# Gated recurrence, then a mixture of experts on one core: experts taken in order with fixed addresses, a branch for the fourth tile, and a new order in the recurrence

## The chip, the cores and the metric

One core of a Trainium2 chip. The metric is the time of one execution on the device in microseconds (us), the median of several runs. Engines are named as in the profile: PE (TensorE matmul), PEld (its weight loads), DVE (VectorE), ACT (ScalarE), POOL (GpSimd), SP (SyncE, which here only issues DMAs). A name with q (SPq, PEldq) is the engine's instruction queue.

## What is computed

Two blocks, one behind the other; everything is 32-bit float.

```python
# recurrence: B=4, H=8, S=768, D=48
f = sigmoid(f_logit)
state = f[t, :, None] * state + outer(k[t], v[t])     # per batch and head
y[t]  = q[t] @ state
# x = y as (B*S, H*D) = (3072, 384)
logits = x @ w_gate                                   # 8 experts
e      = argmax(logits);  gate = softmax(logits)[e]
out    = gate * (relu(x @ w1[e]) @ w2[e])             # F = 1024
```

The inputs come from a fixed seed. Routing them by the reference gives 406, 413, 352, 385, 335, 443, 396 and 342 tokens for experts 0 to 7. In tiles of 128 tokens that is 4, 4, 3, 4, 3, 4, 4 and 3: 29 tiles, five of them fourth ones.

## The kernel before, in words

**Recurrence.** Twelve units (`NU`), each 128 time steps of two batches with all heads, two chains of six. The order on every engine is written out by hand (`manual_schedule`). In iteration `n` of the loop (L434) unit `n` is scored (`score`: PE matmuls, then DVE copies under the causal mask, L298), its keys are transposed (`keys`), the state's increment is made (`added`, PE) and taken up (`update`, DVE and POOL). Unit `n-1` gets its outputs (`within` for the unit's own steps, `before` for the old state, both PE). Unit `n-2` is carried out (`settle`: ACT copies from PSUM; `rows`: PE transposes it and multiplies by the gate's weights, ACT and DVE copy the results). Ahead of that run the gates: `growth(n+2)` (ACT exponent, POOL add), `product(n+2)` (a DVE scan, L258), `by_r(n+1)` (POOL multiplies the keys, L269), `log_r` and `decay` (ACT, with a table load each), `by_decay(n+1)` (DVE, L283). SP loads f, k, q and v of unit `n+3` into one of three buffers each (`ld`, `bufs=3`). The PSUM pool `pst` has two slots, which `xp`, `kp`, `rp` and `dp` take in turn.

**Routing.** Every second iteration, for four chunks of 128 tokens (for two chunks at the end), `Route` chooses the expert (`choose`, DVE), counts by matmul (`count`, PE), computes each token's row in its expert's region (`place`, DVE) and sends four blocks of rows by indirect DMA from POOL to the DRAM array `xs` (`send`, L149).

**Between.** L499 and L500 read a flag on all five engines and branch over a slow fallback that does not run with these inputs. Then SP writes a block of padding rows behind the last token of each expert (L575, L576), while DVE works out a plan of 31 tiles (`NT`, L586 to L615): for each tile its expert and its first row. Tiles that are not needed read a dummy block.

**Experts.** 31 tiles: SP reads expert and row from the plan (L624, L625), loads the rows (`xrow`, L627) and the expert's whole `w1` (`w1t`, 1.5 MB, L629; every tile anew). PE transposes the rows (L633), does 24 matmuls with `w1` (L644; the trace shows 48, two for each in 32-bit float), ACT and DVE each do the relu of one half (L652, L654), PE does 8 matmuls with `w2` (L658; 16 in the trace), reading its expert from a register that L655 loads. DVE scales by the gate (L662) and POOL scatters the rows to the output (L149). All eight `w2` lie in SBUF, loaded during the recurrence. Here the order on the engines is the scheduler's.

Of the kernel before, what the change touches and what calls it, by code (L numbers as in the profile page):

```python
# [19 lines left out]
C = 128  # L20
# [16 lines left out]
DUMMY = E * REGION  # L37
ROWS = DUMMY + C

# [6 lines left out]
NT = N // C + E - 1  # L46
# [5 lines left out]
def _consts():  # L52
# [3 lines left out]
    def row(v):  # L56
# [8 lines left out]
        "eidx": row(e),  # L65
        "tiles": row(np.arange(N // C) * C),
        "i": row(np.arange(NT)),
        "irow": row(np.arange(NT) * C - DUMMY),
# [8 lines left out]
    f["rows"] = sel.reshape(128, HP * XW)  # L77
    m = {"causal": np.triu(np.ones((128, 128)))}
# [17 lines left out]
def kernel(  # L96
# [34 lines left out]
    w2r = cpool.tile([128, E, NF, DM], F32, name="w2r")  # L131
    base = cpool.tile([128, B * NC + 1, E], F32, name="base")
# [12 lines left out]
    nc.scalar.dma_start(xs[DUMMY : DUMMY + C], pad)  # L145
    nc.vector.tensor_copy(base[:, 0], const("first"))
# [14 lines left out]
    class Route:  # L161


        def __init__(self, pool, lg, bases, xr, toks, group):
            self.pool, self.lg, self.bases = pool, lg, bases
            self.xr, self.toks, self.group = xr, toks, group
            self.n = lg.shape[1]
# [22 lines left out]
        def place(self):  # L190
            n, bases, rp = self.n, self.bases, self.rp
            at = self.t("place", E)
            nc.vector.tensor_copy(at[:, 0], bases[0])
# [4 lines left out]
            nc.vector.tensor_tensor(at, rp[:, 0], at, op=OP.add)  # L198
            nc.vector.tensor_tensor(at, at, self.oh, op=OP.mult)
            pos = self.t("pos")  # L200
            nc.vector.reduce_sum(pos, at, axis=AX_X)
            self.posi = self.pool.tile([128, n], I32, name="posi")
            nc.vector.tensor_copy(self.posi, pos)
# [4 lines left out]
        def send(self):  # L208
# [4 lines left out]
            nc.gpsimd.tensor_copy(self.xr[:, :, TOK], self.toks)  # L213
            for c in range(self.n):
                scatter(xs, self.posi[:, c : c + 1], self.xr[:, c, :], ROWS - 1, self.group)


    ordered = {getattr(mybir.EngineType, n) for n in ENGINES}
    with ExitStack() as st:
        ld = st.enter_context(tc.tile_pool(name="ld", bufs=3))  # L220
# [8 lines left out]
        nc.vector.memset(cap[:, :, 0:1], 1.0)  # L229

        scores = [wk.tile([128, 2, 2, HP, C], F32, name=f"at{i}", bufs=1) for i in range(2)]
        for t in scores:
            nc.vector.memset(t, 0.0)
# [4 lines left out]
        def load(u, *names):  # L238
            x = units[u]
            for n in names:  # L240
# [5 lines left out]
                nc.sync.dma_start(x[n], src[u])  # L246

        def growth(u):

            f = units[u]["f"]  # L250
# [3 lines left out]
        def product(u):  # L254

            x = units[u]
            x["r"] = wk.tile([128, SEG, CR], F32, name="r", bufs=1)
            nc.vector.tensor_tensor_scan(  # L258
                x["r"].rearrange("p s c -> p (s c)"),
                x["f"].rearrange("p s c -> p (s c)"),  # L260
                cap.rearrange("p s c -> p (s c)"),
# [5 lines left out]
        def by_r(u):  # L267
            x = units[u]
            nc.gpsimd.tensor_tensor(x["k"], x["k"], x["r"][:, :, 1:CR], op=OP.mult)  # L269
            nc.gpsimd.tensor_copy(rend[:, u], x["r"][:, :, C])  # L270

        def log_r(u):
            x = units[u]
            nc.scalar.activation(x["f"][:, :, 1:CR], x["r"][:, :, 1:CR], AF.Ln)

        def decay(u):
            x = units[u]
            x["dec"] = x["f"][:, :, 1:CR]
            nc.scalar.activation(x["dec"], x["dec"], AF.Exp, scale=-1.0)  # L279

        def by_decay(u):
            x = units[u]
            nc.vector.tensor_tensor(x["q"], x["q"], x["dec"], op=OP.mult)  # L283
# [80 lines left out]
        def update(u):  # L364
# [3 lines left out]
            last = x["dec"][:, :, C - 1 : C].to_broadcast([128, SEG, D])  # L368
# [15 lines left out]
        def rows(u):  # L384
# [3 lines left out]
            if u == g[0]:  # L388
                n = 2 * len(g)
                group["xr"] = wk.tile([128, n, ROW], F32, tag="xr", name="xr")  # L390
                group["lg"] = wk.tile([128, n, E], F32, tag="lg", name="lg")
                nc.gpsimd.memset(group["xr"][:, :, USED:ROW], 0.0)
# [16 lines left out]
            if u != g[-1]:  # L409
                return None  # L410
            n = 2 * len(g)
            b0 = 2 * (g[0] % 2)
            toks = const("tok").rearrange("p (b c) -> p b c", c=NC)[:, b0 : b0 + n, g[0] // 2]
            return Route(
                wk,
                group["lg"],
                [base[:, 2 * g[0] + j] for j in range(n + 1)],
                group["xr"],
                toks,
                "xs",  # L420
            )

        st.enter_context(tc.manual_schedule(engines=ordered))
        for u in range(3):
            load(u, *"fkqv")
        growth(0)
        product(0)
        by_r(0)
        log_r(0)
        decay(0)  # L430
        by_decay(0)
        growth(1)
        product(1)
        for n in range(NU + 2):  # L434
# [7 lines left out]
            if n + 1 < NU:  # L442
                by_r(n + 1)
                log_r(n + 1)
            if 0 <= last:
# [23 lines left out]
            if here < NU and here // 2 < NC - 1:  # L469
                update(here)  # L470
            if rt:
                rt.send()
            if n + 2 < NU:
                product(n + 2)
            if 0 <= back < NU:
                before(back)
            if n + 3 < NU:
                load(n + 3, *"fkqv")
            if 1 <= n <= E:
                e = n - 1  # L480
                nc.sync.dma_start(w2r[:, e], moe_w2[e].rearrange("(f p) d -> p f d", p=128))
# [14 lines left out]
        nc.vector.tensor_copy(end, base[:, B * NC])  # L496
# [3 lines left out]
    with tc.If(flag > 0):  # L500
        with ExitStack() as st:
            gp = st.enter_context(tc.tile_pool(name="gp", bufs=1))
            gps = st.enter_context(tc.tile_pool(name="gps", bufs=1, space=PSUM))
            nc.vector.tensor_copy(end, const("first"))
            wg3 = gp.tile([128, KD, E], F32, name="wg3")
# [42 lines left out]
            with tc.For_i(0, B) as b:  # L548
                with tc.For_i(0, S, C) as c:
# [13 lines left out]
                    rt = Route(gp, lg, [end, end], xr, toks, None)  # L563
                    rt.choose()
                    rt.count(gps.tile([128, 2, 1, E], F32, name="grp"))
                    rt.place()
                    rt.weigh()
                    rt.send()
# [5 lines left out]
    for e in range(E):  # L574
        row = nc.sync.value_load(endi[:, e : e + 1], min_val=e * REGION, max_val=e * REGION + N)  # L575
        ins = nc.sync.dma_start(xs[ds(row, C)], pad).ins  # L576
        tc.declare_no_dep(ins, group="xs", reason="no row is written twice")
        tc.add_to_no_dep_group("xs", ins)


    def p_tile(name, *shape):
        return cpool.tile([1, *shape], F32, name=name)

    one = slice(0, 1)
    cnt = p_tile("cnt", E)
    nc.vector.tensor_tensor(cnt, end[one], const("first")[one], op=OP.subtract)  # L586
    more = p_tile("more", E, N // C)
    nc.vector.tensor_tensor(  # L588
# [131 lines left out]
```

## Time and profile before

| what | us |
| --- | --- |
| median of three runs | 593.29 |
| lowest, highest | 588.04, 596.0 |
| the profiled execution | 593.54 |
| its span in the profile | 591.8 |

The span runs from the first to the last instruction in the trace; the profiled execution's own time is 1.74 us longer. Mean granted TensorE clock over the span: 0.932 of full speed.

### The profile page before, as it was taken

The page shows a single profiled execution, that of the slowest core. Times are in us where ns is not written, and L with a number is a line of the kernel's source. Part 1 is how long each engine was busy: PE and PEld are TensorE (multiplying, and loading weights), DVE is VectorE, ACT ScalarE, POOL GpSimd, SP SyncE. Part 2 cuts the span into 40 slices and gives each one's busy share as a digit, 9 for nine tenths or more (in the row PEclk, how much of TensorE's full clock was granted, in tenths as well). Part 3 has the DMA queues.
Part 4 walks back from the last instruction along what each step waited for, and adds up shares of the span by engine and source line. Part 5 has one row for each costly group of instructions (what it writes and reads, how often), then busy time and mean ns, then how long its engine had stood idle before and what let it go on. Part 6 is the DMA issues. An engine that isn't in the chain of part 4 may idle for free.

```text
span 591.8 us, 9687 instructions
## 1 busy us (share of the span) xinstructions
PE 485.2 (82%) x3803; PEld 396.2 (67%) x3803; DVE 177.0 (30%) x373; ACT 126.0 (21%) x172; POOL 115.2 (19%) x121
## 2 busy tenths in 40 slices
PE   0777957879684049999999999999999999999995
PEld 0767857868574047667867877778667767786683
DVE  5756646667544201112011111110211111202110
ACT  5577546665531001000000000000000000000000
POOL 3333625472723000001000100010001000100010
PEclk9888969979898559999999999999999999999998
DMA  8555686887602483434553555345434544554300
GB/s 336 199 191 215 211 343 208 330 309 251 247 34 77 147 331 115 154 135 138 195 191 126 155 201 177 135 163 191 168 129 157 195 177 135 157 205 162 135 10 0
DMA packets 37665, 105.57 MB, mean 178 GB/s; under 512 B 3806, under 2 KB 17153, under 8 KB 37616
## 3 DMA queue, kind: packets, MB, share of 16 engines
q1 hardware_dynamic: 33248, 94.55, 45.6%
q0 software_dynamic: 3520, 9.64, 4.2%
q10 hardware_dynamic: 848, 0.71, 0.4%
q8 instruction: 32, 0.52, 0.4%
q14 instruction: 17, 0.14, 0.1%
HBM read 93.41 MB, written 12.85 MB: 180 GB/s over the span
## 4 chain that ended last, share of the span: by engine, by line
issue 56%; POOL 5%; PE 2%; SPq 2%; DMA 1%; POOLq 0%; DVE 0%
POOL out_dram L149 5%; PE hps L644 1%; DMA xrow<-xs 1%; PE yps L658 1%; SPq L575 1%; SPq L576 1%; SPq L625 0%; POOLq L149 0%; SPq L624 0%; POOLq L715 0%; SPq L627 0%; SPq L629 0%; DVE ysb L662 0%; DVE more L588 0%; DVE nt L592 0%
## 5 line engine op out<-in xcount | busy, mean ns | idle before, releaser
L644 PEld LDWEIGHTS hps<-xT,w1t 128*128 128x128 f32 x1488 | 172.3, 194 | 21.4 <-DVE xT L635 11.3
L644 PE MATMUL hps<-xT,w1t 128*128 128x128 f32 x1488 | 175.3, 278 | 13.5 <-DVE xT L635 7.8
L658 PE MATMUL yps<-w2r,hT 128*128 x496 | 170.0, 490 | 12.7 <-DVE hT L654 12.5
L658 PEld LDWEIGHTS yps<-w2r,hT 128*128 128x128 f32 x496 | 90.3, 190 | 76.7 <-DVE hT L654 24.4
L149 POOL DMA_INDIRECT out_dram<-ysb,dst x31 | 30.3, 978 | 364.7 <-DVE ysb L662 324.9
L652 ACT ACTIVATE hT<-hps 128x512 f32<-128x512 f32 x31 | 18.5, 597 | 335.5 <-PE hps L644 335.5
L637 DVE CAST dst<-xrow 128x1 int32<-128x1 f32 x31 | 4.8, 154 | 209.3 <-DMA out_dram<-ysb,dst 193.7
L662 DVE TENSOR_SCALAR ysb<-yps,xrow 128x384 f32<-128x384 f32 x31 | 19.1, 617 | 99.2 <-PE yps L658 99.2
L295 PE MATMUL s<-q,k 64*128 64x128 f32 x384 | 28.1, 303 | 19.6 <-DVE q L283 19.6
L295 PEld LDWEIGHTS s<-q,k 64*128 64x128 f32 x384 | 25.8, 211 | 21.3 <-issue 20.6
L258 DVE TENSOR_TENSOR_SCAN r<-f,cap 128x1032 f32<-128x1032 f32 x12 | 32.4, 2703 | 10.1 <-POOL f L252 10.1
L310 PE MATMUL kp<-fpack,k 128*128 128x128 f32 x96 | 18.4, 351 | 20.8 <-DVE lg L404 20.8
L319 PE MATMUL yt<-at,v 128*64 128x128 f32 x384 | 32.0, 328 | 0.0
L397 PE MATMUL xp<-fpack,ys 128*128 128x104 f32 x192 | 26.1, 292 | 7.2 <-ACT ys L380 7.2
L149 POOL DMA_INDIRECT xs<-xr,posi x24 | 26.2, 1094 | 26.1 <-DVE xr L212 13.7
L298 DVE COPY_PREDICATED at<-mpack,s 128x1024 f32<-128x1024 uint8 x24 | 29.6, 1287 | 1.6 <-PE s L295 1.6
L397 PEld LDWEIGHTS xp<-fpack,ys 128*128 128x128 f32 x192 | 24.0, 203 | 9.0 <-ACT ys L380 8.1
L269 POOL TENSOR_TENSOR k<-k,r 128x1024 f32<-128x1024 f32 x12 | 26.2, 2187 | 18.6 <-DVE r L258 14.0
L310 PEld LDWEIGHTS kp<-fpack,k 128*128 128x128 f32 x96 | 14.4, 180 | 23.2 <-DVE lg L404 22.6
L633 PE MATMUL etp<-fpack,xrow 128*128 128x128 f32 x93 | 13.2, 278 | 20.4 <-issue 20.4
L319 PEld LDWEIGHTS yt<-at,v 128*64 128x64 f32 x384 | 27.1, 169 | 3.0 <-issue 2.7
L283 DVE TENSOR_TENSOR q<-q,f 128x1024 f32<-128x1024 f32 x12 | 15.0, 1247 | 44.7 <-ACT f L279 44.7
(81 smaller groups left out, 314.5 us busy)
## 6 DMA issues: line engine op xcount, KB each, us to landing
w1t<-in_moe_w_dram SPq DMA_DIRECT2D x31, 1536.0 KB, 8.1
w2r<-in_moe_w_dram SPq DMA_DIRECT2D x8, 1536.0 KB, 10.0
xrow<-xs SPq DMA_DIRECT2D x31, 200.0 KB, 2.4
f<-in_fu_dram SPq DMA_DIRECT2D x12, 516.0 KB, 7.3
k<-in_ku_dram SPq DMA_DIRECT2D x12, 512.0 KB, 7.9
q<-in_qu_dram SPq DMA_DIRECT2D x12, 512.0 KB, 5.6
v<-in_vu_dram SPq DMA_DIRECT2D x12, 512.0 KB, 5.7
xs<-pad SPq DMA_DIRECT2D x8, 200.0 KB, 1.9
```

What stands on the lines that cost most here:

```text
L149: ins = nc.gpsimd.indirect_dma_start(out=dst, out_offset=bass.IndirectOffsetOnAxis(ap=idx, axis=0), in_=src, in_offset=None, bounds_check= ...
L258: nc.vector.tensor_tensor_scan(x["r"].rearrange("p s c -> p (s c)"), x["f"].rearrange("p s c -> p (s c)"), cap.rearrange("p s c -> p (s c) ...
L269: nc.gpsimd.tensor_tensor(x["k"], x["k"], x["r"][:, :, 1:CR], op=OP.mult)
L295: nc.tensor.matmul(ps[:, h, p], lhsT=x["k"][r, s], rhs=x["q"][r, s], start=True, stop=True)
L298: nc.vector.copy_predicated(x["at"][:, a].rearrange("p h s c -> p (h s) c"), _bc(causal, 1, SEG), ps.rearrange("p h s c -> p (h s) c"),)
L310: nc.tensor.transpose(kp[:, p], x["k"][:, HP * a + p], ident)
L319: nc.tensor.matmul(x["yt"][r, a, p], lhsT=x["v"][:, a, 2 * p + h], rhs=x["at"][:, a, h, p], start=p == 0, stop=x["old"] is None, skip_grou ...
L397: nc.tensor.matmul(xp[:, p], lhsT=x["ys"][:, a, p], rhs=wx[:, p], start=True, stop=True)
L644: nc.tensor.matmul(hp[:, f, :], lhsT=w1t[:, j, o : o + 128], rhs=xT[:, j, :], start=j == 0, stop=j == KD - 1,)
L652: nc.scalar.activation(hT[:, 0:4], hp, AF.Relu)
L658: nc.tensor.matmul(yp, lhsT=hT[:, f, :], rhs=w2r[:, ds(er, 1), f, :], start=f == 0, stop=f == NF - 1)
L662: nc.vector.tensor_scalar(ysb, yp, xt[:, GATE : GATE + 1], None, op0=OP.mult)
```

## The change

- Padding: four tiles' worth of padding rows are written into each of the eight regions in iterations 0 and 1, before any token is sent. The padding after the counts, the plan of 31 tiles and the dummy block go.
- Experts: for each expert in turn three tiles always run, at addresses fixed in advance; all five engines read the expert's last row (`rows_to`), and a fourth tile runs under a branch, with a loop for further tiles under a second one. `w1` and `w2` of an expert are loaded once, three experts deep; the first three during iterations 5, 7 and 9. The order is written by hand: rows are loaded five tiles ahead, and a later tile's transposes (`turn`) stand between the two matmul groups of a tile. `dst` has 7 buffers.
- Recurrence: loads have four buffers, unit 0 is loaded and prepared in halves, the last column of the decay is copied out by POOL (`last`), and the order within an iteration is another. The scatters of a group of four go in twos, one pair at the start of each of the next two iterations. `place` does its running sums by one scan.

```diff
         def place(self):
...
-            for c in range(n):
-                nc.vector.tensor_tensor(bases[c + 1], bases[c], rp[:, 1, c], op=OP.add)
-                if c + 1 < n:
-                    nc.vector.tensor_copy(at[:, c + 1], bases[c + 1])
+            nc.vector.tensor_copy(counts[:, :, 0], self.base)
+            nc.vector.tensor_copy(counts[:, :, 1:], rp[:, 1].rearrange("p n e -> p e n"))
+            nc.vector.tensor_tensor_scan(
+                sums.rearrange("p e n -> p (e n)"),
+                const(f"run{n}"),
+                counts.rearrange("p e n -> p (e n)"),
+                0.0,
+                OP.mult,
+                OP.add,
+            )
...
+    def load_weights(e):
+        w1t = wpool.tile([128, KD, F], F32, name="w1t")
+        nc.sync.dma_start(w1t, moe_w1[e].rearrange("(k p) f -> p k f", p=128))
+        w2t = wpool.tile([128, NF, DM], F32, name="w2t")
+        nc.sync.dma_start(w2t, moe_w2[e].rearrange("(f p) d -> p f d", p=128))
...
+    def load_pads(e):
+        rows = xs[e * REGION : e * REGION + TILES * C]
+        nc.sync.dma_start(
+            rows.rearrange("(t p) r -> p t r", p=C), _bc(pad, 1, TILES)
+        )
...
-        ld = st.enter_context(tc.tile_pool(name="ld", bufs=3))
+        ld = st.enter_context(tc.tile_pool(name="ld", bufs=4))
...
+        load(0, "fkq", ab)
+        load(0, "v")
...
+        for part in ab:
+            growth(0, part)
+        for part in ab:
+            product(0, part)
+        for part in ab:
+            by_r(0, part)
+            log_r(0, part)
+        for t in scores:
+            nc.vector.memset(t, 0.0)
+        for part in ab:
+            decay(0, part)
+            by_decay(0, part)
...
             if n + 1 < NU:
                 by_r(n + 1)
                 log_r(n + 1)
+            if sends:
+                sends.pop(0)()
             if 0 <= last:
                 rt = rows(last)
                 if rt:
                     rt.choose()
-            if here < NU:
-                keys(here)
-            if 0 <= back < NU:
-                within(back, 0)
+            for a in range(2):
+                if 0 <= back < NU:
+                    within(back, a)
             if rt:
                 rt.count(pst.tile([128, 2, rt.n, E], F32, name="rp", **tr))
-            if 0 <= back < NU:
-                within(back, 1)
             if n + 1 < NU:
                 decay(n + 1)
-                by_decay(n + 1)
-            if rt:
-                rt.place()
-            if here < NU:
-                if here // 2 < NC - 1:
-                    added(here)
             if n + 2 < NU:
                 growth(n + 2)
             if rt:
                 rt.weigh()
-            if here < NU and here // 2 < NC - 1:
-                update(here)
+            if n + 1 < NU:
+                by_decay(n + 1)
+            if here < NU:
+                keys(here)
             if rt:
-                rt.send()
+                rt.place()
+                rt.fill()
+                lead["base"] = rt.after
+                if n < NU:
+                    for c in range(0, rt.n, 2):
+                        sends.append(lambda rt=rt, c=c: rt.send(range(c, c + 2)))
+                else:
+                    rt.send(range(rt.n))
             if n + 2 < NU:
                 product(n + 2)
             if 0 <= back < NU:
                 before(back)
+            if here < NU and here // 2 < NC - 1:
+                added(here)
+                update(here)
             if n + 3 < NU:
-                load(n + 3, *"fkqv")
-            if 1 <= n <= E:
-                e = n - 1
-                nc.sync.dma_start(w2r[:, e], moe_w2[e].rearrange("(f p) d -> p f d", p=128))
+                load(n + 3, "fkqv")
+            if n < 2:
+                for e in range(4 * n, 4 * n + 4):
+                    load_pads(e)
+            if n in (5, 7, 9):
+                load_weights((n - 5) // 2)
...
+    def through(x, w, between=()):
+        w1t, w2t = w
...
+        for y in between:
+            turn(y)
...
+    for i in range(5):
+        ahead(i)
+    turn(tiles[0, 0])
+    turn(tiles[0, 1])
+    for e in range(E):
+        w = weights[e]
+        rows_to = nc.values_load(
+            endi[0:1, e : e + 1], min_val=first[e], max_val=first[e] + N
+        )
+        for t in range(TILES - 1):
+            ahead(TILES * e + t + 5)
+            if t == TILES - 2:
+                ahead(TILES * e + t + 6)
+            nexts = [(e, t + 2)] if t < TILES - 2 else [(e + 1, 0), (e + 1, 1)]
+            through(tiles[e, t], w, [tiles[y] for y in nexts if y in tiles])
+        with tc.If(rows_to > first[e] + (TILES - 1) * C):
+            through(tiles[e, TILES - 1], w)
+            with tc.If(rows_to > first[e] + TILES * C):
+                nc.sync.dma_start(xs[ds(rows_to, C)], pad)
+                with tc.For_i(first[e] + TILES * C, first[e] + N, C) as row:
+                    with tc.If(rows_to > row):
+                        x = load_rows(row)
+                        turn(x)
+                        through(x, w)
+        if e + 3 < E:
+            load_weights(e + 3)
```

`turn` is the transposes with their copies out of PSUM (L631 to L637 of before), `through` the rest of a tile (L638 to L663).

## Rows read from the trace of the kernel before

**Rows 1.** Windows: length, busy (instructions) of PE PEld DVE ACT POOL, clock, DMA, GB/s

```profile
0.00:14.30 14.30, 0.00 (x0) 0.00 (x0) 8.09 (x7) 8.38 (x8) 4.42 (x10) 1.00 0.89 333
...
34.49:163.02 128.53, 101.45 (x1321) 93.24 (x1321) 79.74 (x147) 76.30 (x102) 64.31 (x62) 0.87 0.71 257
163.00:190.00 27.00, 19.47 (x232) 17.15 (x230) 12.72 (x68) 7.85 (x17) 7.40 (x11) 0.95 0.12 46
190.00:216.30 26.30, 0.87 (x3) 0.52 (x4) 5.81 (x23) 0.00 (x0) 1.00 (x2) 0.50 0.65 240
216.30:584.50 368.20, 347.67 (x2074) 270.84 (x2074) 56.98 (x120) 19.80 (x32) 29.34 (x30) 0.99 0.44 152
584.50:591.80 7.30, 0.00 (x0) 0.00 (x0) 0.58 (x1) 0.00 (x0) 0.98 (x1) 0.66 0.00 0
```

**Rows 2.** Windows: the last two tiles of the expert stage, same columns

```profile
563.12:584.46 21.34, 21.30 (x128) 16.71 (x128) 2.41 (x4) 1.19 (x2) 1.71 (x2) 1.00 0.02 7
```

**Rows 3.** Waits, 216 to 585 us: who waited for whom; total, times, longest

```profile
DVE dst L637 <- DMA out_dram<-ysb,dst: 193.7, 28, 7.9
...
PE yps L658 <- DVE hT L654: 12.5, 17, 1.5
```

**Rows 4.** Timeline, the transposes of two tiles in the expert stage: start, length

```profile
419.03 0.82 PE L633 MATMUL etp<-fpack,xrow 128*128 128x128 f32 x6
```

**Rows 5.** Lines L655 and L500: count, ns min/median/max, first and last start

```profile
L655 PEldq TENSOR_LOAD <-plani x31: 294/301/576, 196.3 to 276.3; - x31
L655 PEldq FUSED_REGOPS  x31: 146/146/165, 196.7 to 276.7; - x31
...
L500 PEldq COMPARE_BRANCH  x1: 356/356/356, 190.3 to 190.3; - x1
```

**Rows 6.** Waits of the whole span

```profile
PEld etp L633 <- issue: 23.1, 16, 20.4
...
DVE endi L573 <- DVEq L500: 1.0, 1, 1.0
```

**Rows 7.** Timeline between the last scatter and the first expert matmul

```profile
190.32 0.98 POOL L149 DMA_INDIRECT xs<-xr,posi  x1 [0.30 <-DVE end L496]
...
216.31 8.15 PE L644 MATMUL hps<-xT,w1t 128*128 128x128 f32 x48 [5.76 <-DVE dst L637]
```

**Rows 8.** DMA issues of the page: KB each, median us from issue to landing

```profile
xrow<-xs SPq DMA_DIRECT2D x31, 200.0 KB, 2.4
...
xs<-xr,posi POOLq DMA_INDIRECT x24, 5.1
...
mpack<-c_mpack ACTq DMA_DIRECT2D x1, 16.0 KB, 2.5
```

**Rows 9.** Waits, 30 to 165 us

```profile
PE kp L310 <- DVE lg L404: 20.6, 9, 3.9
...
PE xp L397 <- ACT ys L380: 5.7, 2, 3.9
```

**Rows 10.** Timeline, PE of one iteration of the recurrence, 108 to 121 us

```profile
108.10 2.06 PE L295 MATMUL s<-q,k 64*128 64x128 f32 x32
...
110.08 2.03 PE L397 MATMUL xp<-fpack,ys 128*128 128x104 f32 x16
...
113.60 1.09 PE L310 MATMUL kp<-fpack,k 128*128 128x128 f32 x8 [1.49 <-DVE lg L404]
...
116.21 1.09 PE L319 MATMUL yt<-at,v 128*64 128x128 f32 x16
117.13 1.09 PE L355 MATMUL dp<-v,kn 128*64 128x48 f32 x32
118.15 1.95 PE L339 MATMUL yt<-q,state 48*48 48x128 f32 x32
```

**Rows 11.** Timeline, unit 0: the first exponent and the last step before `score`

```profile
4.79 1.06 ACT L251 ACTIVATE f<-f 128x1032 f32<-128x1032 f32 x1 [1.36 <-DMA f<-in_fu_dram]
...
12.96 1.23 DVE L283 TENSOR_TENSOR q<-q,f 128x1024 f32<-128x1024 f32 x1 [3.49 <-ACT f L279]
```

More of the change, by code (lines that the diff above doesn't have):

```diff
@@ L77, in _consts @@
     f["rows"] = sel.reshape(128, HP * XW)
+    for n in (1, 2, 4):
+        f[f"run{n}"] = row(np.tile(np.arange(n + 1) > 0, E))
     m = {"causal": np.triu(np.ones((128, 128)))}
@@ L229 @@
         nc.vector.memset(cap[:, :, 0:1], 1.0)
+        lead = {"base": const("first")}
         scores = [wk.tile([128, 2, 2, HP, C], F32, name=f"at{i}", bufs=1) for i in range(2)]
-        for t in scores:
-            nc.vector.memset(t, 0.0)
         units = [{} for _ in range(NU)]
@@ L410, in rows @@
                 return None
[L411 to L421, printed above, removed]
-        st.enter_context(tc.manual_schedule(engines=ordered))
[L424 to L431, printed above, removed]
+            return Route(wk, group["lg"], lead["base"], group["xr"], "xs")
+        st.enter_context(tc.manual_schedule(engines=ordered))
+        ab = (slice(0, HP), slice(HP, SEG))
+        load(0, "fkq", ab)
+        load(0, "v")
+        load(1, "fkqv")
+        load(2, "fkqv")
+        for part in ab:
[10 more added lines that the diff above has]
+            by_decay(0, part)
         growth(1)
         product(1)
+        sends = []
         for n in range(NU + 2):
@@ L495 @@
         nc.vector.tensor_copy(badi, bad)
-        nc.vector.tensor_copy(end, base[:, B * NC])
+        nc.vector.tensor_copy(end, lead["base"])
     flag = nc.values_load(badi[0:1, 0:1], min_val=0, max_val=1)
@@ L566 @@
                     rt.place()
+                    nc.vector.tensor_copy(end, rt.after)
                     rt.weigh()
-                    rt.send()
+                    rt.fill()
+                    rt.send([0])
                     nc.vector.tensor_scalar(toks, toks, float(C), None, op0=OP.add)
@@ L573 @@
     nc.vector.tensor_copy(endi, end[0:1])
[L574 to L588, printed above, removed]
[L589 to L618 removed]
+    xp = ctx.enter_context(tc.tile_pool(name="xp", bufs=7))
     ep = ctx.enter_context(tc.tile_pool(name="ep", bufs=2))
@@ L658, with ahead @@
             nc.tensor.matmul(
-                yp, lhsT=hT[:, f, :], rhs=w2r[:, ds(er, 1), f, :], start=f == 0, stop=f == NF - 1
+                yp, lhsT=hT[:, f, :], rhs=w2t[:, f, :], start=f == 0, stop=f == NF - 1
             )
         ysb = ep.tile([128, DM], F32, name="ysb", bufs=3)
-        nc.vector.tensor_scalar(ysb, yp, xt[:, GATE : GATE + 1], None, op0=OP.mult)
-        scatter(out, dst, ysb, N - 1, "out")
+        nc.vector.tensor_scalar(ysb, yp, x["x"][:, GATE : GATE + 1], None, op0=OP.mult)
+        scatter(out, x["dst"], ysb, N - 1, "out")
+    first = [e * REGION for e in range(E)]
+    order = [(e, t) for e in range(E) for t in range(TILES)]
+    tiles = {}
+    def ahead(i):
+        if i < len(order):
+            e, t = order[i]
+            tiles[e, t] = load_rows(slice(first[e] + t * C, first[e] + t * C + C))
+    ctx.enter_context(tc.manual_schedule(engines=ordered))
+    for i in range(5):
+        ahead(i)
+    turn(tiles[0, 0])
+    turn(tiles[0, 1])
+    for e in range(E):
+        w = weights[e]
+        rows_to = nc.values_load(
+            endi[0:1, e : e + 1], min_val=first[e], max_val=first[e] + N
+        )
+        for t in range(TILES - 1):
[15 more added lines that the diff above has]
+            load_weights(e + 3)
 _OUTS = [((N, DM), "float32")]
```

147 lines of the change are left out of this document (63 added, 84 removed).

## The prediction

> **What bounds the kernel now.** I read a table of windows first, with its cuts where one kind of work ends and the next begins [rows 1]. It shows a recurrence in which PE is busy for 101.45 of 128.53 us, a gap of 26.3 us (190.0 to 216.3) with almost no PE work, and an expert stage of 368.2 us in which PE is busy for 347.67. So PE sets the expert stage, nothing that computes sets the gap, and in the recurrence PE waits a fifth of the time. Then, for each of the three, I read who waits for whom: in the expert stage the two last tiles, which run without a stall [rows 2], against the waits of the stage [rows 3]; in the gap the queues of PE [rows 5, 6] and the timeline [rows 7]; in the recurrence PE's two large waits [rows 9] and the order of one iteration [rows 10].
>
> **Expert stage.** Two tiles without a stall take 21.34 us, 10.67 each [rows 2]; the transposes of two tiles take 0.82, so 0.41 each [rows 4]. The first `w1` group runs at the lower clock (0.50 of full speed in the gap [rows 1]) and takes 8.15 [rows 7] where half of 10.67 is usual: 2.8 more. Then 31 x (10.67 + 0.41) + 2.8 = 346.3, near the 347.67 busy; the other 20.5 of 368.2 are stalls. Most are PE waiting for DVE's half of the relu, 12.5 us in 17 waits, and DVE is late because the copy of `dst` ahead of it waits for a scatter to the output to release its buffer, 193.7 us in 28 waits [rows 3]. Seven `dst` buffers instead of three end that, and transposes between the two groups mean that PE no longer waits for `xT`. So I take all stalls as gone. Late next is PE itself.
>
> The tokens make 29 tiles, not 31, and all 32 possible tiles are transposed, two of them before the first matmul: 29 x 10.67 + 30 x 0.41 + 2.8 = 324.5. The weights cost nothing: an expert's 3 MB come once per 33 us or more, where before 1.5 MB came per tile with a DMA share of 0.44 [rows 1].
>
> Added are the branches. On every engine an expert now ends in a branch, and the next begins with a register load. The trace has both, once each in another place. The branch at L500 held DVE for 1.0 us from the end of one operation to the start of the next [rows 6]; on PE the compare alone was 0.36, and a register load with its arithmetic is 0.30 + 0.15 [rows 5]. Behind the branch wait PE's next `w1` group and, through it, everything; DVE, ACT and POOL pass their own branches in the time of the first group, SP has five tiles of rows and two experts' weights ahead. From below the price is 0: the register loads of the present stage run to 276.3 us beside a busy PE [rows 5]. From above it is a DMA for the code at the target: the smallest transfer in the trace of such a size, 16 KB, landed after 2.5 us [rows 8], so 4.0 with the rest. I take 1.0 + 0.45 = 1.5, nearest to the rows of the same instructions, and count seven between eight experts: 10.5.
> New stage: 335.0, against 368.2: **33.2 less**.
>
> The Trainium skill speaks against the branches here: "Runtime: NRT & Kernel Launch", section "Instruction fetch mechanics", says that code reaches an engine in blocks of 16 KiB, fetched in sequence, and that a branch to code not fetched yet must first wait for a DMA. At L500 the trace shows no such wait (0.36 for PE's compare, 1.0 for the whole crossing on DVE); by that rule each of eight branches could cost a fetch, and the sum would be that of the second rival.
>
> **The gap.** PE's first transpose waits 20.4 us for nothing but its own queue [rows 6]: most of its 31 register loads, 0.45 each [rows 5], stand ahead of it and wait for the plan. Behind that comes `w1`, to 216.3 [rows 7]. Plan, padding and loads of registers go, and the first weights are there. Late next is the last scatter: it starts at 190.32 [rows 7], lands 5.1 later, then the row load takes 2.4 [rows 8] and about 0.3 of issue, then two tiles are transposed at 0.87 each (the lower clock's length; the one wait behind the flag's branch is over by then). First `w1` matmul at about 199.9 instead of 216.3: **16.4 less**. Bounds: 13 less if the first loads queue behind each other, 19 less if the scatter lands as fast as a row load.
>
> **Recurrence.** In the nine iterations from 34.5 to 163.0 PE idles 27.1 us [rows 1]. Of that, 20.6 are nine waits at `kp` for a PSUM slot that DVE's `lg` must release, and 5.7 are two waits at `xp`, where ACT stands still behind an f that has not landed [rows 9]. The new order puts both `within` groups (2 x 1.09 [rows 10]) between `xp` and `keys`: up to 2.2 of each wait of 2.3 on average is covered, at most 19.6 in all; with waits up to 3.9 some remain and short ones leave cover unused, so I count four fifths, 16. The fourth load buffer ends the 5.7. Against that, in four iterations with routing `kp`'s second half now takes the slot of `rp`, which `place` reads behind `by_decay`: one such operation (1.23 [rows 11]) and a small one, 1.4 each, 5.6 in all. Sum **16 less**. Bounds: 27 less if PE never idles, none if the wait only moves to the gates on ACT and DVE, each busy for 76 to 80 of the 128.5 us [rows 1]. The scatters in twos and the shorter `place` cost nothing on this path; `last` is one small POOL copy a unit beside 64 us of POOL work in 128.5. The padding (6.6 MB) and the first three experts' weights (9.4 MB) replace 12.6 MB of `w2`; the 3.4 MB more are 10 us of DMA at 333 GB/s, beside a share of 0.71 [rows 1]. That is hidden; if not, f is late again for some 5.7.
>
> **Start and end.** In halves each of some five handovers between the first exponent and the last step before the first score (8.2 us apart, steps of 1.06 to 1.23 [rows 11]) comes half a step earlier, 2.7, of which the clearing of the score buffers, now in between on DVE, takes some back: **2 less**, bounds 0 and 3. The tail from 163 to 190 stays: its chain of two last units has the same steps. At the end POOL passes a branch behind its last scatter: **1 more** [rows 6].
>
> **Sum.** The profiled execution took 593.5, as good as the median of 593.3. 593.5 - 33.2 - 16.4 - 16 - 2 + 1 = 526.9, so 527.
>
> **Rivals.**
> - The recurrence keeps its pace, since its waits move to the gates or the loads compete with the padding: 527 + 16 = 543. For it: the gates' engines are busy for 60%, and their steps follow one another. Against it: the wait at `kp` is for an order, not for work. Chance 0.18.
> - Every branch fetches its code: 8 x 2.5 more, 547. For it: eight jumps over two tiles' and a loop's code. Against it: L500 shows 1.0. With no fetch seen in the trace, 0.17. (The rule of the Trainium skill quoted above would lead here.)
> - PE never idles: 11 less in the recurrence, and the branches hide: 10.5 less, 505. Chance 0.10.
> - On the other side: the branch acts as a full drain. The last operations of the kernel show one: 7.3 us from the last matmul to the end [rows 1], because the last scatter must land. If all engines met so at each of eight experts, and PE restarted at the lower clock each time (2.8), it were 10.1 each, 81 in place of 10.5: 597, slower than before. It decides from 9.6 us a branch (66.6 + 10.5, over 8). Against it: at L500 each engine went on by itself, though scatters were in flight. Chance 0.04.
> The forecast keeps 0.51.
>
> **Range and chances.** From 506 (third rival) to 555 (either of the first two, and half of the other). A measurement of this kernel tells about 2% from no change, that is 11.9 us. All cases but the drain are faster by over 2%: with odds and ends 0.94 faster, 0.04 within, 0.02 slower.
>
> **What would show it.** Right: first `w1` matmul about 10 us after the last scatter starts; 29 tiles of 11.1 us with no wait for the relu; a PE gap of about 1.5 us at each expert; the score-to-score distance down from 14.3 to about 12.5. Wrong: PE gaps of 4 us or more at the experts, PE's clock falling in them, `kp` still waiting for `lg`, f still late, or the recurrence ending as late as 190.

## The result and the profile after

The changed kernel takes **508.49 us** (median; 506.96 to 509.52) against 590.66 for the kernel before on the same chip: a ratio of 0.860, 95% interval 0.852 to 0.867. The profiled execution took 506.96, its span is 505.1.

The table of windows of the changed kernel, cut where one kind of work ends (columns as in [rows 1]: length, busy time and instructions of PE, PEld, DVE, ACT, POOL, clock, DMA share, GB/s):

```profile
0.00:15.10 15.10, 0.00 (x0) 0.03 (x1) 8.62 (x8) 9.35 (x11) 7.73 (x14) 1.00 0.90 328
15.10:33.10 18.00, 14.38 (x176) 13.12 (x176) 13.01 (x11) 12.95 (x16) 11.32 (x11) 0.91 1.04 392
33.13:134.13 101.00, 92.98 (x1324) 84.40 (x1320) 73.02 (x123) 76.85 (x101) 60.14 (x69) 0.95 0.86 325
134.13:163.40 29.27, 19.50 (x232) 17.53 (x230) 11.71 (x58) 7.84 (x17) 8.91 (x13) 0.90 0.15 57
163.40:173.16 9.76, 1.51 (x7) 1.17 (x7) 0.91 (x4) 0.00 (x0) 0.98 (x1) 0.50 0.52 149
173.16:497.90 324.74, 317.63 (x1946) 253.56 (x1946) 54.08 (x120) 18.60 (x30) 27.28 (x28) 1.00 0.23 81
497.90:505.10 7.20, 0.00 (x0) 0.00 (x0) 0.12 (x1) 0.00 (x0) 0.97 (x1) 0.82 0.05 20
```

Against [rows 1], the recurrence's row shows the same PE work (1324 recorded instructions, 1321 before) in 101.00 instead of 128.53 us: PE's idle part fell from 27.1 to 8.0, and its busy part from 101.45 to 92.98, at a clock of 0.95 instead of 0.87. The gap with almost no PE work fell from 26.3 to 9.76. By the starts of the first `score` of each unit, of the flag's matmul, of the first `w1` matmul and of the last `ysb` (the scaling by the gate) in the two traces, the two spans divide without a remainder:

| stage | before | after | change | forecast |
| --- | --- | --- | --- | --- |
| start to first `score` | 14.33 | 15.11 | +0.8 | -2 |
| two first iterations | 20.16 | 18.02 | -2.1 | none given |
| nine iterations | 128.53 | 101.00 | -27.5 | -16 |
| tail, to the flag's matmul | 25.75 | 27.78 | +2.0 | 0 |
| gap, to the first `w1` matmul | 27.54 | 11.25 | -16.3 | -16.4 |
| experts, to the last `ysb` | 368.15 | 324.24 | -43.9 | -33.2 |
| end | 7.34 | 7.70 | +0.4 | +1 |

The timeline of the changed kernel, last scatter on POOL, then PE at the first experts (start, length):

```profile
163.46 0.98 POOL L145 DMA_INDIRECT xs<-xr,posi  x1 [0.30 <-DVE end L536]
...
171.49 1.51 PE L633 MATMUL etp<-fpack,xrow 128*128 128x128 f32 x6 [9.03 <-DMA xrow<-xs]
173.16 6.42 PE L647 MATMUL hps<-xT,w1t 128*128 128x128 f32 x48 [0.16 <-DVE dst L637]
...
184.90 5.52 PE L647 MATMUL hps<-xT,w1t 128*128 128x128 f32 x48
...
195.75 5.52 PE L647 MATMUL hps<-xT,w1t 128*128 128x128 f32 x48
...
206.93 5.52 PE L647 MATMUL hps<-xT,w1t 128*128 128x128 f32 x48
...
218.67 5.60 PE L647 MATMUL hps<-xT,w1t 128*128 128x128 f32 x48 [1.06 <-DVEq L696]
```

The first `w1` matmul starts 9.7 us after the last scatter (25.99 in [rows 7]). A tile with one tile's transposes takes 10.85 (184.90 to 195.75), with two tiles' 11.18. Nothing waits between tiles until the branch at 217.6. Its wait is in the waits of the whole span (who waited for whom; total, times, longest), the branch's own instructions on PE's queue are in the views of L696 and L685 (count, ns min/median/max), and the loads of instructions are in the DMA queues of a window, here 213 to 216 us of the changed kernel and 190 to 193 of the kernel before (packets, MB, share):

```profile
PE hps L647 <- DVEq L696: 4.9, 5, 1.1
PE hps L647 <- DVEq L694: 1.6, 2, 0.8
```
```profile
L696 PEldq COMPARE_BRANCH  x10: 174/206/334, 213.3 to 464.2; - x10
...
L685 PEldq TENSOR_LOAD <-endi x8: 298/306/319, 171.5 to 464.4; - x8
```
```profile
q8 instruction: 1, 0.02, 1.8%
...
q8 instruction: 1, 0.02, 2.5%
```

L696 ends a fourth tile that ran, L694 one that was skipped: together 6.5 us at seven experts, 0.93 each. The name DVEq only says which signal came last: in this wait PE's queue runs a compare and the register load of its own.

The two q8 lines are blocks of 16 KB of instructions. The first starts at 214.31, 1.0 us after PE's queue reached the compare at 213.31; the matmuls ahead of that compare run until 217.6.

### The profile page after: what moved, and what is told of

The parts are those of the page before. It is cut to its first block, busy times and chain, and to the rows that moved or that the text cites. A ratio compares the mean times of both kernels' runs of the same rounds, so it can differ in the third digit from the quotient of the medians.

```text
span 505.1 us, 8779 instructions
## 1 busy us (share of the span) xinstructions
PE 446.0 (88%) x3678; PEld 369.8 (73%) x3678; DVE 161.5 (32%) x321; ACT 125.6 (25%) x173; POOL 117.3 (23%) x135
## 4 chain that ended last, share of the span: by engine, by line
issue 57%; PE 21%; ACT 7%; POOL 6%; DVE 4%; DMA 2%; another core or an unknown queue 1%; POOLq 1%; SPq 0%; DVEq 0%; ACTq 0%
POOL out_dram L145 5%; PE s L325 4%; PE xp L430 4%; PE yt L369 4%; PE dp L385 2%; ACT L305 2%; PE yt L349 2%; ACT f L305 2%; PE kp L340 1%; DMA xs<-xr,posi 1%; DVE r L282 1%; PE hps L647 1%; ACT f L274 1%; PE yps L662 1%
## 5 line engine op out<-in xcount | busy, mean ns | idle before, releaser
L647 PEld LDWEIGHTS hps<-xT,w1t 128*128 128x128 f32 x1392 | 160.2, 193 | 16.8 <-PEq L696 7.9
L647 PE MATMUL hps<-xT,w1t 128*128 128x128 f32 x1392 | 161.5, 276 | 6.7 <-DVEq L696 4.9
L662 PE MATMUL yps<-w2t,hT 128*128 128x384 f32 x464 | 154.5, 486 | 0.0
L662 PEld LDWEIGHTS yps<-w2t,hT 128*128 128x128 f32 x464 | 85.9, 190 | 53.8
L655 ACT ACTIVATE hT<-hps 128x512 f32<-128x512 f32 x29 | 17.3, 597 | 294.6 <-PE hps L647 294.6
L657 DVE TENSOR_SCALAR hT<-hps 128x512 f32<-128x512 f32 x29 | 20.1, 692 | 148.1 <-PE hps L647 148.1
L325 PE MATMUL s<-q,k 64*128 64x128 f32 x384 | 29.5, 313 | 15.1 <-POOL last L308 15.1
L325 PEld LDWEIGHTS s<-q,k 64*128 64x128 f32 x384 | 27.0, 221 | 15.9 <-POOL last L308 15.1
L282 DVE TENSOR_TENSOR_SCAN r<-f,cap 128x1032 f32<-128x1032 f32 (+1 forms) x13 | 28.7, 2207 | 12.4 <-POOL f L275 12.4
L294 POOL TENSOR_TENSOR k<-k,r 128x1024 f32<-128x1024 f32 (+1 forms) x13 | 26.4, 2031 | 2.5 <-DVE r L282 2.4
L349 PE MATMUL yt<-at,v 128*64 128x128 f32 x384 | 23.6, 276 | 0.0
L633 PE MATMUL etp<-fpack,xrow 128*128 128x128 f32 x96 | 15.1, 282 | 9.0 <-DMA xrow<-xs 9.0
L369 PE MATMUL yt<-q,state 48*48 48x128 f32 x320 | 21.2, 286 | 0.0
L635 DVE COPY xT<-etp 128x384 f32<-128x384 f32 x32 | 17.4, 548 | 8.0 <-PE etp L633 8.0
```

The source lines that it names most:

```text
L282: nc.vector.tensor_tensor_scan(x["r"][:, part].rearrange("p s c -> p (s c)"), x["f"][:, part].rearrange("p s c -> p (s c)"), cap[:, part]. ...
L294: nc.gpsimd.tensor_tensor(k, k, r[:, :, 1:CR], op=OP.mult)
L325: nc.tensor.matmul(ps[:, h, p], lhsT=x["k"][r, s], rhs=x["q"][r, s], start=True, stop=True)
L349: nc.tensor.matmul(x["yt"][r, a, p], lhsT=x["v"][:, a, 2 * p + h], rhs=x["at"][:, a, h, p], start=p == 0, stop=x["old"] is None, skip_grou ...
L369: nc.tensor.matmul(x["yt"][r, a, p], lhsT=x["old"][r, HP * a + p], rhs=x["q"][r, HP * a + p], start=False, stop=True, skip_group_check=True,)
L647: nc.tensor.matmul(hp[:, f, :], lhsT=w1t[:, j, o : o + 128], rhs=x["xT"][:, j, :], start=j == 0, stop=j == KD - 1,)
```

## The experiments

Each is the changed kernel or the kernel before with one edit, the last one with three. The median of before beside them was 593.5 to 595.5 us, beside the changed kernel 590.66. So a total that differs from 508.49 by less than some 5 us shows little by itself, and the stages in the traces decide.

### Expert stage: branch, buffers, dummy tiles

**The five fourth tiles written out**, without a branch or register load:

```diff
-        rows_to = nc.values_load(...)
-        with tc.If(rows_to > first[e] + (TILES - 1) * C):
+        if e in (0, 1, 3, 5, 6):
             through(tiles[e, TILES - 1], w)
```

> The changed kernel with its branches and register loads taken out of the expert stage; the five fourth tiles are written out where these inputs need them, so it computes the same for them, but for no other counts. If a branch costs PE the gap seen in the trace, seven gaps of about 0.93 us go: 6.5 us less, about 502. If the gaps only stand where PE would wait anyway, it stays at 508. If branches also cost something elsewhere (code loading, late engines), it falls below 498.

Measured: 500.42 us (496.59 to 501.62), 8.1 below the changed kernel. Its timeline, PE from the third tile to the next expert's second:

```profile
198.48 5.52 PE L647 MATMUL hps<-xT,w1t 128*128 128x128 f32 x48
203.84 0.82 PE L633 MATMUL etp<-fpack,xrow 128*128 128x128 f32 x6
209.65 5.52 PE L647 MATMUL hps<-xT,w1t 128*128 128x128 f32 x48
220.17 5.52 PE L647 MATMUL hps<-xT,w1t 128*128 128x128 f32 x48
```

A tile without transposes takes 10.52 (209.65 to 220.17), one with two tiles' transposes 11.17, so a tile's transposes cost 0.33. The stage, 175.88 to 491.89, is 316.0 long, 8.2 less than the changed kernel's. So the seven branches between experts cost 1.2 us each there. The end, behind the eighth, is 0.6 shorter (7.11 against 7.70).

**Seven `dst` buffers in the kernel before:**

```diff
-            dst = ep.tile([128, 1], I32, name="dst", bufs=3)
+            dst = ep.tile([128, 1], I32, name="dst", bufs=7)
```

> The kernel before with seven buffers for dst instead of three, nothing else. If DVE's wait for a scatter to release dst makes the relu late, PE's 12.5 us of waits for the relu go from the expert stage: 576 to 583 beside a kernel before of 593. If something else makes DVE late, the stage stays at 368 us.

Measured: 578.64 us, a ratio of 0.984 whose interval (0.966 to 1.003) just includes 1; the expert stage of its trace, 217.40 to 566.79, is 349.4 long, 18.8 less. The waits of that stage say why:

```profile
DVE dst L637 <- DMA xrow<-xs: 61.1, 29, 4.2
...
PE hps L644 <- DVE xT L635: 7.8, 15, 0.5
```

The wait of `dst` for the scatter to the output [rows 3] and the wait of PE for `hT` are gone; 7.8 us of PE waiting for `xT` are left, which the changed kernel's place for the transposes removes. PE idles 12.6 less, about what it had waited for `hT` (12.5). Its busy time fell as well, from 347.67 to 341.56; 1.2 of this is the first `w1` group (6.97 instead of 8.15).

**Two tiles fewer in the kernel before:**

```diff
-NT = N // C + E - 1
+NT = N // C + E - 3
```

> The kernel before with 29 expert tiles in its loop instead of 31: the two left out hold no token, so only their share of the time is missing. Theory (each tile costs its place in the stage, 11.1 to 11.9 us: stall-free work of 10.67 plus its part of the transposes and waits): 23 us less than the kernel before, about 572 us. Rival (the last tiles overlap the end or the store, so that they cost less): 577 to 585 us.

Measured: 571.33 us against 593.45 beside it, 22.1 less: 11.1 for each tile that held no token. The ratio of 0.965 (0.954 to 0.977) leaves 14 to 27 us for the two; in the traces the expert stage is 26.1 shorter (219.15 to 561.17, 342.0).

### Recurrence: order, buffers, clock

**The keys before both `within`** (the old place of `keys`, the rest of the new order kept):

```diff
+            if here < NU:
+                keys(here)
             for a in range(2):
                 if 0 <= back < NU:
                     within(back, a)
...
-            if here < NU:
-                keys(here)
```

> The changed kernel with the key transposes back ahead of the unit's own outputs, as in the kernel before; all else as changed. If the order of these two is what took PE's idle time away, the wait of the key transposes for the logits returns (20 us in nine iterations), the nine iterations grow by 16 to 27 us, their granted clock falls from 0.95 towards 0.87, and the time is 524 to 535. If the split scatters and the fourth buffer did it, the time stays within 5 us of 508.

Measured: 519.98 us (519.71 to 522.06), 11.5 more than the changed kernel. Its row of windows for the nine iterations, and its waits there:

```profile
33.83:146.92 113.09, 96.19 (x1320) 86.98 (x1321) 71.65 (x123) 77.43 (x104) 63.41 (x69) 0.94 0.76 288
```
```profile
PE kp L340 <- DVE lg L437: 10.6, 9, 1.3
```

The nine waits at `kp` are back with 10.6 us, half of their 20.6 [rows 9]. The iterations are 12.1 longer, below the 16 to 27 expected: PE idles 8.9 more and is busy for 3.2 more.

**Three load buffers instead of four:**

```diff
-        ld = st.enter_context(tc.tile_pool(name="ld", bufs=4))
+        ld = st.enter_context(tc.tile_pool(name="ld", bufs=3))
```

> The changed kernel with three load buffers instead of four. If the late f cost what it showed before, ACT waits for f again, 5 to 6 us reach PE, with some loss of clock: 513 to 518. If the new order leaves enough time for three buffers, it stays at 508.

Measured: 535.10 us (534.96 to 535.61), 26.6 more than the changed kernel and far above the 513 to 518 expected. The row of windows for the nine iterations, the waits in the recurrence, and the timelines of SP and ACT:

```profile
34.29:163.50 129.21, 102.63 (x1324) 93.53 (x1320) 73.03 (x123) 76.66 (x101) 60.50 (x69) 0.84 0.75 280
```
```profile
ACT f L274 <- DMA f<-in_fu_dram: 25.2, 4, 9.1
...
PE dp L385 <- ACT kn L341: 19.2, 4, 7.4
```
```profile
103.13 0.33 SPq L267 DMA_DIRECT2D q<-in_qu_dram  x1
...
103.98 0.43 SPq L229 DMA_DIRECT2D w1t<-in_moe_w_dram  x1
104.45 0.49 SPq L231 DMA_DIRECT2D w2t<-in_moe_w_dram  x1
105.05 5.05 SPq L267 DMA_DIRECT2D f<-in_fu_dram  x1
...
120.08 1.06 ACT L274 ACTIVATE f<-f 128x1032 f32<-128x1032 f32 x1 [9.10 <-DMA f<-in_fu_dram]
```

SP in the changed kernel, the same f:

```profile
82.63 4.17 SPq L267 DMA_DIRECT2D f<-in_fu_dram  x1
```

The nine iterations take 129.21, as long as before the change: with three buffers the whole gain of the recurrence is gone. The q and v of unit `n+3` wait until `within(n)` and `before(n)`, an iteration later, give up their buffers, and SP stands there. Then come 3 MB of weights or four regions of padding, and the next f lies behind these on the same queue. ACT waits for an f four times, 25.2 us in all: twice behind weights (9.1 and 8.3, at 120.08 and 149.67) and twice behind padding (5.8 and 1.9). It then stands in front of `kn`, which `dp` needs. In the changed kernel the wait for f is 1.2 us, once. There, too, each f lies behind the weights, but the whole chain of loads runs an iteration earlier: this f is issued 15.7 us before ACT takes it up (82.63 and 98.30), with three buffers 5.9 us before ACT is ready for it. A kernel before with four buffers was not tried.

**The count and `place` behind `before` and `product`:**

```diff
-            if rt:
-                rt.count(pst.tile([128, 2, rt.n, E], F32, name="rp", **tr))
...
-            if rt:
-                rt.weigh()
...
             if rt:
+                rt.weigh()
+            if 0 <= back < NU:
+                before(back)
+            if n + 2 < NU:
+                product(n + 2)
+            if rt:
+                rt.count(pst.tile([128, 2, rt.n, E], F32, name="rp", **tr))
                 rt.place()
                 rt.fill()
...
```

(`before` and `product` are taken out of their old places behind it; the sends follow `fill` as they did.)

> The changed kernel with the counts, place and fill behind before and product in the iteration, so that the second half of the key transposes takes a slot that no count holds. If that wait (1.3 us in each iteration with routing) and the clock that falls behind it are what is left there, iterations with routing come down from 12.0 to about 11.2 and none shows the lower clock: 498 to 504. If DVE is the bound there, scan and place only change places and the time stays at 508 or grows by 2.

Measured: 503.51 us (503.31 to 503.99), 5.0 below the changed kernel; the nine iterations take 96.60. Its row of windows:

```profile
33.71:130.31 96.60, 89.48 (x1325) 81.07 (x1321) 68.73 (x123) 75.82 (x101) 58.45 (x65) 1.00 0.89 335
```

The waits at `kp` are gone, and so is something else. This is PE's timeline of the changed kernel in one iteration:

```profile
49.52 0.63 PE L340 MATMUL kp<-fpack,k 128*128 128x128 f32 x4
51.59 0.71 PE L340 MATMUL kp<-fpack,k 128*128 128x128 f32 x4 [1.44 <-DVE place L201]
52.24 3.65 PE L369 MATMUL yt<-q,state 48*48 48x128 f32 x32
```

And these are two of its windows there, the wait and what follows:

```profile
50.20:51.59 1.39, 0.00 (x0) 0.03 (x1) 1.29 (x6) 0.89 (x1) 0.61 (x1) 1.00 1.01 398
...
52.24:55.89 3.65, 3.65 (x35) 3.21 (x36) 3.06 (x3) 0.69 (x2) 0.67 (x1) 0.50 0.87 345
```

The matmuls with the old state, 1.95 elsewhere [rows 10], take 3.65 here, at the lower of the two clocks (0.50), right behind a wait of 1.44 before which the clock was 1.00. That iteration takes 15.1 us (part of it a late f), the three others with routing 12.0. In the kernel with the late count PE does not wait at `kp`, and the clock is 1.00 over all nine iterations. But most of the waiting has only moved, to the next iteration's `xp`:

```profile
PE xp L430 <- DVE place L201: 2.8, 3, 1.0
...
PE xp L430 <- DVE state L402: 2.5, 7, 0.4
```

PE idles 7.1 us there, against 8.0; its busy part fell by 3.5. From score to score, the three later pairs of iterations (one with routing, one without) take 0.5 us more each than in the changed kernel. The whole gain, 5.9, lies in the first pair (42.60 to 69.63 there, 43.18 to 64.35 here), the one with the lower clock. Whether the missing wait kept the clock up or an f that came earlier (ACT waits 0.6 for it, not 1.2) is not separated.

**The scatters at once**, four in a row in the iteration that makes them:

```diff
-                if n < NU:
-                    for c in range(0, rt.n, 2):
-                        sends.append(lambda rt=rt, c=c: rt.send(range(c, c + 2)))
-                else:
-                    rt.send(range(rt.n))
+                rt.send(range(rt.n))
```

> The changed kernel with all four scatters of a group sent at once, at the end of the iteration that routes them. If POOL is off the path, as the prediction has it, within 2 us of 508. If four scatters in a row (5.2 us) hold up the next unit's key product, the four iterations behind a routing one grow by 2 to 5 us each: 516 to 528.

Measured: 512.20 us (507.05 to 512.29). One execution is as fast as the changed kernel, the others are some 4 us slower; the profiled one has two iterations of 14.1 and 15.4 us at a lower clock. Whether the scatters bring that about is open; the rival's 516 and more are not there. Beside its own before the ratio is 0.857 (0.849 to 0.864), no worse than the changed kernel's 0.860. The tail's row of windows, first `score` of the last unit to the flag's matmul, shows that the twos have a price:

```profile
141.69:166.71 25.02, 18.51 (x230) 16.64 (x229) 11.25 (x55) 7.92 (x17) 6.44 (x10) 0.96 0.13 50
```

With the scatters at once the tail takes 25.02 us, 2.8 less than the 27.78 of the changed kernel.

**The padding in four iterations instead of two:**

```diff
-            if n < 2:
-                for e in range(4 * n, 4 * n + 4):
+            if n < 4:
+                for e in range(2 * n, 2 * n + 2):
                     load_pads(e)
```

> The changed kernel with the padding written in iterations 0 to 3, two regions each, instead of 0 and 1. If the padding ahead of f makes the iteration of unit 3 long (15.1 us against 12.0 for the later ones with routing), that iteration falls to about 12 and the time by 2 to 5 us. If its length comes from the wait for the slot of the counts alone, nothing changes.

Measured: 513.23 us (511.43 to 516.88), 4.7 more, where 2 to 5 less were expected; the nine iterations of its trace take 104.1 (34.63 to 138.72), 3.1 more. The iteration of 15.1 us fell to 12.03, as expected, but a later one took 20.3 (65.95 to 86.27). Waits of 30 to 140 us, and POOL's timeline:

```profile
POOL xs L145 <- issue: 10.9, 14, 7.8
...
DVE r L282 <- POOL f L275: 12.1, 5, 7.9
```
```profile
68.24 1.18 POOL L145 DMA_INDIRECT xs<-xr,posi  x1 [7.80 <-issue]
...
71.06 1.07 POOL L275 TENSOR_SCALAR f<-f 128x1032 f32<-128x1032 f32 x1
```

The scatter of 68.24 stood on POOL for 7.8 us, with the next unit's gate behind it, and the scan waited for that gate (7.9). This view names only "issue" as what released it. The semaphore records of the same trace name the padding: its last block was issued at 56.51 and had landed at 67.32, and POOL's wait for that block's semaphore ended at 67.35. So padding in advance is free only while it lands before the first scatter.

### Start and tail

**Unit 0 whole instead of in halves:**

```diff
-        load(0, "fkq", ab)
-        load(0, "v")
+        ab = (whole,)
+        load(0, "fkqv")
```

> The changed kernel with unit 0 loaded and prepared whole, as before. If halves save time, the first score comes 1 to 2 us later than 15.1. If the second half of f, which lands at 6.5 behind the others, makes halves useless, it comes at the same time or earlier; the total stays within 1 us either way.

Measured: 508.17 us (505.53 to 512.64), the same; the first `score` comes at 14.47 instead of 15.11. The halves gain nothing. ACT's timeline of the changed kernel shows the reason:

```profile
3.71 0.63 ACT L274 ACTIVATE f<-f 128x516 f32<-128x516 f32 x1 [0.78 <-DMA f<-in_fu_dram]
5.62 0.91 ACTq L137 DMA_DIRECT2D fpack<-in_moe_w_gate_dram  x2
6.57 0.63 ACT L274 ACTIVATE f<-f 128x516 f32<-128x516 f32 x1 [2.23 <-DMA f<-in_fu_dram]
```

The first half is exponentiated 1.1 us earlier than the whole in [rows 11], but the second starts only at 6.57, when the whole had been done (4.79 and 1.06). By its DMA records that half landed at 5.76; then ACT's own queue issued two loads of the gate's weights, until 6.53.

**The late count, three row buffers (`xr`), and no `keys` for the last two units:**

```diff
-                group["xr"] = wk.tile([128, n, ROW], F32, tag="xr", name="xr")
+                group["xr"] = wk.tile([128, n, ROW], F32, tag="xr", name="xr", bufs=3)
...
-            if here < NU:
+            if here < NU and here // 2 < NC - 1:
                 keys(here)
```

> The count placed behind the product, as in the kernel with the late count (503.5 us), and two more edits: three buffers for the rows instead of two, and no transposes of the keys for the last two units, whose keys no update reads. In the tail ScalarE waited 5.3 to 5.7 us for the row buffer that late scatters still read. Theory (that wait is on the path that ends the tail): the tail falls from 27.7 to 22 to 24 us and the last two scoring iterations lose some 1 us, so the time is 496 to 500 us. Rival (the wait lies beside the chain of the next group's counting, or the scatters on POOL are late next): the tail stays above 26 us and the time is 501 to 505 us.

Measured: **497.48 us** (496.98 to 497.97), a ratio of 0.843 to before (0.836 to 0.849), below both kernels. The tail's row of windows, first `score` of the last unit to the flag's matmul:

```profile
129.89:152.44 22.55, 17.34 (x220) 15.88 (x221) 11.37 (x55) 6.71 (x15) 9.45 (x16) 0.98 0.20 74
```

That is 22.55, against 27.78 in the changed kernel and 27.70 with the late count alone (130.31 to 158.01). Of the 5.2 between this run and the late count alone, 1.0 lies ahead of the last unit's `xp`, where the keys stood, and 4.1 behind it. ACT's copies of the last unit's rows, first in the changed kernel and then in this one:

```profile
156.47 0.86 ACT L433 COPY xr<-xp 128x384 f32<-128x384 f32 x2 [3.27 <-DMA xs<-xr,posi]
```
```profile
146.17 0.48 ACT L433 COPY xr<-xp 128x384 f32<-128x384 f32 x1 [0.74 <-PE xp L430]
```

The wait for a scatter to release the row buffer (3.27 here, 5.7 with the late count alone) was on the path, and with a third buffer PE alone is waited for.

## Why the prediction was right, and where it was not

The forecast was 527, the result lies 18.5 lower, inside the range; direction and the three causes held. By its steps:

- **The gap** (-16.4 forecast, -16.3 measured) is right in size and way: the plan, the padding and the register loads went, and the chain from the last scatter over the row load to the transposes is what is left, 9.7 us.
- **The expert stage** was forecast at 335.0 and is 324.2; the mechanism held, each price was too high. The stall-free tile, taken from the last two [rows 2], was 10.67 and measures 10.52: 4.3 us on 29 tiles. That window runs to the start of the last tile's scaling, so it holds the way from PE to DVE, which nothing hides there, and is 0.3 more than two tiles. The transposes, 0.41, measure 0.33: 2.4. The slow first group, 2.8, measures 0.9 (6.42 against 5.52): 1.9. The branches, 7 x 1.5 = 10.5, measure 8.2: 2.3. Together 10.9, for the 10.8 that the stage came out lower. That most stalls were DVE's `dst` was right (12.6 of the 20.5 idle us go with the seven buffers, the other 7.8 are waits for `xT`); that PE's busy time falls with them was not in the sum. That a dropped tile is worth its whole time agrees with the 11.1 of the medians, within the wide interval of that run.
- **The branches** are not what the second and fourth rival feared. The longest PE wait at one is 1.1 us, far from the 10.1 of a drain, and the clock of the stage is 1.00. But the prediction's "no fetch seen in the trace" was a misreading. The trace of before has one: PE's compare at L500 starts at 190.35, and a block of 16 KB of instructions at 191.38. In the changed kernel such a block starts 1.0 to 1.6 us behind seven of PE's eight jumps over code. The rival's mechanism is there; what is not there is its price. PE's queue reaches the jump about 4.3 us before the matmuls ahead of it end (213.31 and 217.6), and the block, about 1 us long, is loaded by then. The Trainium skill's rule on fetched code ("Runtime: NRT & Kernel Launch", section "Instruction fetch mechanics") has a DMA fetch before execution goes on as the price of a branch whose target is not there yet. This trace agrees on the fetch, and shows no wait of PE for it. The 1.1 us of waiting hold a second compare (0.19 at the first such branch) and the register load (0.31), and skipping a tile or not makes little difference (0.8 on average behind L694, 1.0 behind L696).
- **The recurrence** was forecast 16 shorter and is 27.5 shorter. In idle time the forecast was near: PE idles 19.1 less (27.1 to 8.0). The term that was not there at all is the rest: I took PE's busy time as fixed, but 8.5 of the 27.5 are the same matmuls at a higher clock. The split failed too. I gave the order 16 and the fourth buffer 5.7. Without the new place of the keys the iterations take 12.1 more, without the fourth buffer 28.2 (18.6 idle, 9.6 busy). These are not shares that add up: each run takes one part out of the finished kernel. That the padding and the weights stay hidden on SP's queue held, but only by the fourth buffer: with three, ACT waits 25.2 us for f behind them.
- **The new wait on `rp`'s slot** was forecast at 1.4 in four iterations, 5.6. Waits of 5.3 are there, but only one of them, 1.4, is for `place`. In the three others (3.9) the second half of the keys waits for ACT's copy of the first half (`kn`), and `place` reads `rp` only later (79.03, where the matmuls at `kp` go on at 78.13). That the sum came so near is luck. Moving the count away gave 5.0; in the nine iterations 3.5 of 4.4 are PE's busy time, at the higher clock.
- **The tail** was taken as unchanged and is 2.0 longer. The step that failed is that its chain "has the same steps": the scatters in twos reach into it (POOL starts the last of four in a row at 156.34), and ACT's copy of the last unit's rows waits 3.3 us for a scatter. With the scatters at once that wait is gone and the tail is 2.8 shorter; a third row buffer, with the keys of the last units left out, takes 5.2 off.
- **The start** was forecast at -2 and is +0.8. The step that failed is that every handover comes half a step earlier: that needs the input to be there, and f's second half landed 1.0 us after the whole f had been taken up before, and was taken up 0.8 later still, behind ACT's own issues. The clearing of the score buffers took its part, as said: it held DVE until 14.41, while the exponent that `by_decay` needs had ended at 13.26.

The third rival's time, 505, came nearest, but not by its way: PE still idles 8.0 us in the recurrence and 6.5 at the branches. The first rival, a recurrence that keeps its pace since the loads compete, is what the run with three buffers shows.

## What to carry to other kernels

When PE idles often in a stage, price its busy time too: idle time that goes takes low-clock time with it. When a large transfer is put on a queue, look at what stands behind it in order and when that is needed; one more buffer can be worth more than the reordering beside it. When a wait is taken out, look for it at the next place that needs the same slot. A step moved to run in advance, like the padding, needs a landing time as well as a bandwidth.

## What was not expected of the hardware

- The same 1324 matmuls in the same order took 92.98 us at a mean clock of 0.95 and 102.63 at 0.84 (three buffers), and nearly the same 1325 took 89.48 at 1.00 (late count).
- The clock went from 1.00 to 0.50 right behind a short wait in a busy stretch: in the changed kernel behind one of 1.44 us, in the run without branches once behind 1.29 us (the matmuls with the old state then took 3.61 instead of 1.95). Other waits of 1.3 us were not followed by a fall, and neither were two of 1.83 us in the run with three buffers. What decides is open.
- An f of 516 KB behind 3 MB of weights on one queue kept ACT waiting for up to 9.1 us, though the DMA engines' mean busy share over the nine iterations was only 0.75; from the issue of those weights to the end of that wait (103.98 to 120.08) it was 0.97.
- Blocks of 16 KB of instructions are loaded behind jumps while PE works off what is queued ahead: behind seven of PE's eight jumps one started 1.0 to 1.6 us after the compare, and the longest wait of PE at a branch was 1.1 us.
